# Three blocks per pass, attention of block 1 by DMA transposes, and products of a constant between the H products

## The chip, the cores and the metric

One core of one Trainium2 chip runs the whole program. The metric is the device time of one execution in microseconds (us), as a median of several executions. The engines are TensorE (PE, its weight loads PEld), VectorE (DVE), ScalarE (ACT), GpSimd (POOL) and SyncE (SP), which here only issues DMA transfers.

## The reference

Attention without softmax, RMS norm, and two layers of "mixture" form; everything is float32 in and out.

```python
# q, k, v: 4 batches x 8 heads x 576 positions x 64
kv = einsum('bhsd,bhse->bhde', k, v);  out = einsum('bhsd,bhde->bhse', q, kv)
x = out / sqrt(mean(out*out, -1) + 1e-6) * g_norm       # -> 2304 tokens x 512
h = x @ w_in                                            # 512 x 2048
y = (h * tanh(softplus(h))) @ w_out                     # 2048 x 512
h2 = y @ w2_in                                          # 512 x 1024
z = h2 * softmax(h2);  ln = (z - mean) / sqrt(var + 1e-6) * g_ln
result = ln @ w2_out                                    # 1024 x 512
```

## The kernel before

The 2304 tokens are six blocks of 384. A float32 value is carried as two fp16 parts, high and low, and each product is three fp16 products (high*high, high*low, low*high). A weight matrix arrives in pieces of 512 KB (W1, the first layer's `w_in`, and W2, its `w_out`, 16 pieces each; W3 and W4 for the second layer). Each piece is decoded into its parts by seven steps on three engines: `w_scale` and `w_hi` on ACT, `w_sign` on POOL, `w_low`, `w_put` and `w_lo` on DVE. Five stage buffers hold pieces under way, so a later load on SP waits for the `w_put` of the piece five before it.

PE's work, in order: for each block the attention; "H" products (`h_mm`), 12 matmuls for 128 rows of the hidden layer, 16 such products per block; "Y" products (`y_mm`), also 12 matmuls each; then per tile of 128 tokens a "2" product (`emit_H2`, 24 matmuls of 512 columns) and an "O" product (`emit_O`, the same size), with the layer norm of the tile between them on DVE, ACT and POOL and its result turned by a DMA transpose (`s_T`, tile `lnT`) on the way to O.

Blocks 0 and 1 have their attention in an early form (the functions `e_...`): q is transposed on PE against a unit matrix (`qTp`), multiplied by kv in float32 (`xoT`), mean squares and the norm's factors go through PE as well (`rT`), and the result lands transposed as the two parts `xT` that H reads. Blocks 2 to 5 use the functions `a_...`: q is split on ACT and DVE, turned by a DMA transpose (`qT`), multiplied (`xo`), normed, split, and turned by a second DMA transpose into `xT`. kv itself (`kv_pair`, tile `kvp`) is a sum over positions: 96 partitions of 6 positions, two heads side by side in the 128 columns of the array.

Blocks 0 and 1 first run with the first half of W1 and W2, then with the second half; a partial Y sum is parked by `y_part` on ACT and added later. All other blocks run through whole.

The order on every engine is written by a planner (`Plan.order`). Each task has an engine, a cost in us, the tasks it follows and a lag; PE tasks have due times from a nominal line of H, Y, 2 and O products. The planner takes, per engine, the ready task with the earliest due time, and the instructions stand in the order of the planned times. On the chip each engine then works in that order, whatever the times turn out to be. Before the first H product, gaps in PE's plan of over 1 us get products of zeros (`keep_warm`).

Of the kernel before, what the change touches and what calls it, by code (L numbers as in the profile page):

```python
# [32 lines left out]
class Plan:  # L33
    def __init__(self):
        self.tasks = {}

# [3 lines left out]

    def order(self):
        tasks = self.tasks
        index = {k: n for n, k in enumerate(tasks)}
        followers = {k: [] for k in tasks}
        for k, t in tasks.items():
            for a in t[3]:
                followers[a].append(k)

        seen, topo = set(), []

        def visit(k):
            stack = [(k, iter(tasks[k][3]))]
            seen.add(k)
            while stack:
                at, it = stack[-1]
                for a in it:
                    if a not in seen:
                        seen.add(a)
                        stack.append((a, iter(tasks[a][3])))
                        break  # L60
                else:
                    topo.append(at)
                    stack.pop()

        for k in tasks:
            if k not in seen:
                visit(k)
        due = {}
        for k in reversed(topo):
            d = 1e9 if tasks[k][5] is None else tasks[k][5]  # L70
            for f in followers[k]:
                d = min(d, due[f] - tasks[k][1] - tasks[k][4])
            due[k] = d
        waits = {k: len(t[3]) for k, t in tasks.items()}
# [8 lines left out]
        while True:  # L83
            best = None
            for e, ks in open_.items():
                if ks:
                    at = max(free[e], min(ready[k] for k in ks))
                    if best is None or at < best[0]:
                        best = (at, e)
            if best is None:  # L90
                break
            at, e = best
# [5 lines left out]
            for f in followers[k]:  # L98
                waits[f] -= 1
                ready[f] = max(ready[f], end + tasks[k][4])  # L100
                if not waits[f]:
                    open_[tasks[f][0]].append(f)
        assert len(out) == len(tasks), [k for k in tasks if waits[k] > 0][:20]
# [4 lines left out]
def tile_attn_moe_moe2(  # L108
# [76 lines left out]
    yorder = [(0, 0), (0, 1), (1, 0), (1, 1), (0, 2), (0, 3), (1, 2), (1, 3)]  # L185
    yorder += [(b, g) for b in range(2, NB) for g in range(4)]
# [29 lines left out]
    def load_q(b):  # L216
# [37 lines left out]
    HALF = [slice(0, 64), slice(64, 128)]  # L254

    def kv_full(b, i):

        c = slice(i, i + 1) if b == 0 else slice(0, 4)
        nc.scalar.activation(
            out=kvf[b][HALF[0], c, HALF[0]], in_=kvp_t[b][HALF[0]], func=ACTF.Copy)  # L260
        nc.vector.tensor_copy(out=kvf[b][HALF[1], c, HALF[1]], in_=kvp_t[b][HALF[1]])

    def kv_zero():
        nc.gpsimd.memset(kvr[0], 0.0)

    def kv_hi(b):
        for o in HALF:
            nc.scalar.activation(
                out=kvr[b % 2][o, 0, :, o], in_=kvp_t[b][o], func=ACTF.Copy, scale=32.0)

    def kv_lo(b):
        p = kvp_t[b]
        for o in HALF:
            nc.vector.scalar_tensor_tensor(
                out=kvr[b % 2][o, 1, :, o], in0=p[o], scalar=32.0,
                in1=kvr[b % 2][o, 0, :, o], op0=ALU.mult, op1=ALU.subtract,
# [22 lines left out]
    def e_xo(b, c):  # L299
        qT = eq_t.pop((b, c)).rearrange("p (r t) -> p r t", r=R)  # L300
        p = ex_t[b, c] = psY.tile([128, BLK], FP32, tag=f"y{c % 3}", name="xoT")
        p = p.rearrange("p (r t) -> p r t", r=R)
        for lo, hi, bb in ((0, 128, 0),) if b == 0 else ((0, 64, 0), (64, 128, 1)):
            nc.tensor.matmul(  # L304
                out=p[:, :, lo:hi], lhsT=kvf[bb][:, c], rhs=qT[:, :, lo:hi], start=True, stop=True)
# [6 lines left out]
    def e_ms(b, c):  # L312
        p, tag = (psH, "h") if b == 0 else ((psA, "a"), (psY, "y3"))[c % 2]
        er_t[b, c] = p.tile([128, 512], FP32, tag=tag, name="rT")
# [75 lines left out]
    def a_xo(b, r):  # L390
        qT = qT_t.pop((b, r))
        p = psA.tile([128, H, D], FP32, tag="a", name="xo")
# [157 lines left out]

    def h_mm(b, grp, i, only=None):
        f = (grp * G + i) * 128
        if (b, grp, i) not in h_t:
            h_t[b, grp, i] = psH.tile([128, BLK], FP32, tag="h", name="hp")
# [29 lines left out]
    def y_ends(b, grp):  # L584
        first = grp == 0 or (b < 2 and grp == 2)
        last = grp == 3 or (b < 2 and grp == 1)
# [34 lines left out]
    def y_hi(b, c):  # L621
        if b < 2:
# [5 lines left out]
    def y_lo(b, c):  # L628
        if b < 2:
# [144 lines left out]
    LAND = 1.9  # L774
    load_after = {}

    for n, u in enumerate(PIECES):
        opened = ("open",) if u[0] in "34" else None
        if n < NST:
            before = [("ld", ("1", 0))] if n else [("ld", 0, 3)]  # L780
            before = before[:1] if n >= 0 else [("ldq", 0)]
        else:
            before = [("put", PIECES[n - NST])]
        task(("ld", u), "S", 1.65, w_load, (u,), before + [opened], LAND)
# [23 lines left out]
    KV1 = ("ld", ("1", 3))  # L808
# [7 lines left out]
    for b in range(B):  # L816
        for i in range(4):
            free = []
            if b == 0 and i:
                free = [("ld", 0, i - 1)]  # L820
            if b == 1:
                free = [("ld", 1, i - 1) if i else KV1]
                free += [("kv", 0, i - 2)] if i > 1 else []
            if b == 2:
                free = [("kv", 0, i), ("kv", 1, i + 2) if i < 2 else None]
                free += [("put", ("2", 7))]
            if b == 3:
                free = [("kv", 2, i), ("put", ("2", 15))]
            task(("ld", b, i), "S", 1.8, load_pair, (b, i), free, LAND)

    ring("qhl", 3, ("xo", 1, 3))
    for i in range(4):
        task(("kv", 0, i), "P", 0.9, kv_pair, (0, i),
             [("ld", 0, i)] + ring("a", 1, ("kvf", 0, i)), 0.25)
        task(("kvf", 0, i), "A", 0.3, kv_full, (0, i), [("kv", 0, i), ("zero",)], 0.2)
    for b in range(2):
        task(("ldq", b), "A" if b == 0 else "S", 0.5 if b == 0 else 2.5, load_q, (b,),
             [("qT", 0, c) for c in range(4)] + [KV1] if b else [], 5.0 if b == 0 else LAND)
        if b == 1:
# [246 lines left out]
```

## Time and profile before

| what | us |
|---|---|
| median of 3 runs (640.6 to 642.23) | 641.05 |
| the profiled execution | 646.7 |
| its span, first to last instruction | 644.9 |
| PE busy in the span | 624.8 |

The profiled execution is 1.8 us longer than its span. The page's slices divide the span into 40 stretches of 16.1 us and give the busy share in tenths; the granted clock is 10/10 at 2.4 GHz and 5/10 at 1.2 GHz. A chain of waits follows the last instruction back, at each step to what released it. In a timeline the number in brackets is the idle time of the engine just before the row, and who ended it.

### The profile page before, as it was taken

To read this page: it belongs to the slowest core of one execution; us is meant where nothing else is said; L and a number is where in the kernel's file an instruction comes from. 1 tells how busy PE (TensorE), PEld (TensorE's weight loads), DVE (VectorE), ACT (ScalarE), POOL (GpSimd) and SP (SyncE) were. 2 spreads that over 40 slices of the span, in tenths; PEclk is the share of its full clock that TensorE was granted. 3 is DMA by queue.
4 is the path that set the end of the run, shared out by engine and by line. 5 is a ranking of instruction groups with operands and counts; after the bars stand their busy time and mean duration, and the time that the engine had idled before them with its cause. 6 is when DMAs were issued, how large, how long until landed. Compare 5 with 4: busy or idle time off the path is not lost.

```text
span 644.9 us, 9802 instructions
## 1 busy us (share of the span) xinstructions
PE 624.8 (97%) x4010; PEld 355.0 (55%) x4010; DVE 307.7 (48%) x529; ACT 269.2 (42%) x461; POOL 93.1 (14%) x125
## 2 busy tenths in 40 slices
PE   7899998999999999999999999999999999999995
PEld 5557564666666666666666656665444444444441
DVE  0667887921633144212321239952835555455540
ACT  2568756541523243422332247642523433433340
POOL 1516422100200022001200122500000000000000
PEclk9989798999999999999999999999999999999998
DMA  9985497365340025002200055500342232324322
GB/s 258 270 223 180 134 290 216 80 134 145 66 82 1 1 50 79 4 0 42 41 2 2 17 180 171 188 1 1 66 99 49 66 82 66 83 65 99 77 71 65
DMA packets 92605, 60.41 MB, mean 94 GB/s; under 512 B 65680, under 2 KB 86160, under 8 KB 92560
## 3 DMA queue, kind: packets, MB, share of 16 engines
q1 hardware_dynamic: 91360, 59.00, 36.6%
q10 hardware_dynamic: 1200, 0.79, 0.4%
q8 instruction: 31, 0.51, 0.3%
q14 instruction: 14, 0.11, 0.1%
HBM read 39.33 MB, written 4.72 MB: 68 GB/s over the span
## 4 chain that ended last, share of the span: by engine, by line
PE 89%; DMA 6%; DVE 2%; ACT 2%; issue 1%; POOL 1%; SPq 0%; DVEq 0%; ACTq 0%; POOLq 0%
PE hp L557 27%; PE y L597 26%; PE op L757 15%; PE h L674 14%; DMA st<-in_moe_w_in_dram 2%; PE kvp L246 2%; DMA st<-in_moe_w_out_dram 1%; PE qTp L288 1%; PE xo L398 1%; DMA yT<-in_v_dram 1%; DMA xT<-xhl 1%; PE xoT L304 1%; PE rT L337 1%; DMA lnT<-hl 1%; PE rT L317 1%
## 5 line engine op out<-in xcount | busy, mean ns | idle before, releaser
L597 PE MATMUL y<-g,w 128*128 128x384 f16 x1152 | 204.7, 330 | 2.5 <-ACT yT L610 2.5
L557 PE MATMUL hp<-xT,w 128*128 128x384 f16 x1152 | 201.3, 327 | 3.0 <-ACT w L533 1.9
L597 PEld LDWEIGHTS <-w 128*128 128x128 f16 x1152 | 112.6, 99 | 78.8 <-issue 6.5
L557 PEld LDWEIGHTS <-w 128*128 128x128 f16 x1152 | 111.7, 98 | 78.6 <-ACT w L533 2.2
L567 ACT ACTIVATE m<-hp 128x384 f32<-128x384 f32 x96 | 46.9, 488 | 132.5 <-PE hp L557 131.9
L757 PE MATMUL op<-w,lnT 128*128 128x512 f16 x432 | 97.7, 384 | 4.2 <-DMA lnT<-hl 4.2
L579 DVE SCALAR_TENSOR_TENSOR g<-m,g 128x768 f16<-128x768 f32 x48 | 46.7, 973 | 110.6 <-ACT g L574 110.5
L674 PE MATMUL h<-w,yT 128*128 128x512 f16 x432 | 96.2, 379 | 0.0
L757 PEld LDWEIGHTS <-lnT 128*128 128x128 f16 x432 | 42.6, 99 | 56.5 <-DMA lnT<-hl 4.7
L674 PEld LDWEIGHTS <-yT 128*128 128x128 f16 x432 | 42.3, 98 | 50.4
L510 POOL TENSOR_SCALAR st<-st 128x512 f32<-128x512 f32 x48 | 42.7, 895 | 91.7 <-ACT P L505 71.3
L515 DVE SCALAR_TENSOR_TENSOR st<-st 128x512 int32<-128x512 int32 x48 | 37.1, 787 | 16.8 <-POOL st L510 16.8
L574 ACT ACTIVATE g<-m 128x768 f16<-128x768 f32 x48 | 40.4, 841 | 1.8 <-PE y L597 0.8
L691 ACT ACTIVATE e<-h,nb 128x1024 f32<-128x1024 f32 x18 | 20.1, 1114 | 48.9 <-DVE nb L686 44.4
L505 ACT ACTIVATE P<-st 128x512 f32<-128x512 f32 x48 | 31.9, 673 | 14.2 <-DMA st<-in_moe_w_out_dram 7.8
L522 DVE SCALAR_TENSOR_TENSOR P<-P,st 128x512 int32<-128x512 int32 x48 | 35.6, 759 | 0.2
L418 POOL TENSOR_SCALAR ms<-ms 128x8 f32<-128x8 f32 x12 | 2.6, 216 | 228.2 <-DVE ms L413 228.2
L698 DVE SCALAR_TENSOR_TENSOR z<-h,e 128x1024 f32<-128x1024 f32 x18 | 22.0, 1225 | 21.4 <-ACT e L691 21.4
L724 POOL TENSOR_SCALAR var<-var 128x1 f32<-128x1 f32 x18 | 3.4, 190 | 192.6 <-DVE var L719 192.6
L738 ACT ACTIVATE hl<-z 128x1024 f16<-128x1024 f32 x18 | 19.0, 1056 | 28.9 <-DVE z L733 28.9
L705 ACT ACTIVATE e<-z,nmz 128x1024 f32<-128x1024 f32 x18 | 20.7, 1147 | 23.7 <-DVE nmz L701 23.7
L742 DVE TENSOR_TENSOR hl<-z,hl 128x1024 f16<-128x1024 f32 x18 | 22.0, 1224 | 15.7 <-ACT hl L738 15.7
(96 smaller groups left out, 421.6 us busy)
## 6 DMA issues: line engine op xcount, KB each, us to landing
st<-in_moe_w_in_dram SPq DMA_DIRECT2D x24, 512.0 KB, 6.7
st<-in_moe_w_out_dram SPq DMA_DIRECT2D x24, 512.0 KB, 4.3
yT<-in_k_dram SPq DMA_DIRECT2D x16, 288.0 KB, 7.9
yT<-in_v_dram SPq DMA_DIRECT2D x16, 288.0 KB, 8.1
out_dram<-osb SPq DMA_DIRECT2D x18, 256.0 KB, 2.0
qraw<-in_q_dram SPq DMA_DIRECT2D x3, 768.0 KB, 6.3
qraw<-in_q_dram SPq DMA_DIRECT2D x4, 384.0 KB, 8.6
qraw<-in_q_dram ACTq DMA_DIRECT2D x1, 768.0 KB, 6.9
```

The lines of the kernel that those rows point to most:

```text
L505: nc.scalar.activation(out=P, in_=v[:, :, 1], func=ACTF.Copy, scale=2.0 ** -111)
L510: nc.gpsimd.tensor_scalar(out=v[:, :, 1], in0=v[:, :, 1], scalar1=0.0, scalar2=1.0, op0=ALU.mult, op1=ALU.mult)
L515: nc.vector.scalar_tensor_tensor(out=v[:, :, 0], in0=v[:, :, 0], scalar=29, in1=v[:, :, 1], op0=ALU.logical_shift_right, op1=ALU.bitwise_or)
L522: nc.vector.scalar_tensor_tensor(out=P.bitcast(I32), in0=P.bitcast(I32), scalar=3, in1=v[:, :, 0], op0=ALU.logical_shift_left, op1=ALU.bit ...
L557: nc.tensor.matmul(out=h_t[b, grp, i], lhsT=w1[:, c, wa, f:f + 128], rhs=xT_t[b][:, C * xa + c], start=(c == 0 and m == 0), stop=(c == C - ...
L567: nc.scalar.activation(out=m_t[b, grp, i // 2][:, i % 2], in_=h_t.pop((b, grp, i)), func=ACTF.Mish, scale=2.0 ** -16)
L574: nc.scalar.activation(out=g_t[b, grp][:, 0, 2 * i:2 * i + 2], in_=m_t[b, grp, i], func=ACTF.Copy, scale=64.0)
L579: nc.vector.scalar_tensor_tensor(out=g_t[b, grp][:, 1, j], in0=m_t.pop((b, grp, i)), scalar=64.0, in1=g_t[b, grp][:, 0, j], op0=ALU.mult, ...
L597: nc.tensor.matmul(out=y_t[cc][:, 0:BLK], lhsT=w2[:, grp * G + ii, wa, cc * 128:(cc + 1) * 128], rhs=g_t[b, grp][:, ga, ii], start=(first ...
L674: nc.tensor.matmul(out=hp[:, half], lhsT=y[:, c, ya, tok], rhs=w3[:, c, wa, half * 512:(half + 1) * 512], start=(m == 0), stop=(m == 3 * C ...
L698: nc.vector.scalar_tensor_tensor(out=z, in0=T[t, "hp"], scalar=2.0 ** -14, in1=T[t, "e"], op0=ALU.mult, op1=ALU.mult, accum_out=sz)
L757: nc.tensor.matmul(out=op, lhsT=lnT[:, K2 * la + kk], rhs=w4[:, kk, wa], start=(m == 0), stop=(m == 3 * K2 - 1),)
```

## The change

Block 1's attention takes the form `a_...`; only block 0 keeps the early form. k and v are laid on 128 partitions of 9 positions, one head of a pair on partitions 0 to 63 and the other on 64 to 127 (`load_pair`, `kv_pair`). Three blocks instead of two (`NI = 3`) run through the first half of the weights before the second half, and Y follows H's order of blocks. The first loads on SP stand in a fixed line, q of block 0 first. The planner runs twice, the second time with the first plan's times as due times. `keep_warm` multiplies the unit matrix, 256 columns at a time, and now also fills planned gaps of over 0.5 us after the first H product, up to a planned time of 150, in the bank of the next H product.

```diff
+    NI = 3
...
-    units = [(0, 0), (0, 1), (1, 0), (1, 1), (0, 2), (1, 2), (0, 3), (1, 3)]
-    units += [(b, g) for b in range(2, NB) for g in range(4)]
...
-    line = ["H", "H", "H", "Y", "H", "Y", "Y"]
+    units = [(b, 2 * half + g) for half in range(2) for b in range(NI) for g in range(2)]
+    units += [(b, g) for b in range(NI, NB) for g in range(4)]
+    line = ["H", "H", "H"]
     while line.count("H") < NU:
-        line += ["H", "Y"]
-    hs, ys = iter(units), iter(yorder)
+        line += ["Y", "H"]
+    hs, ys = iter(units), iter(units)
...
-        t = yT[(0 if b == 1 else 2) + i].rearrange("p c a t -> p (c a t)").bitcast(FP32)[0:KP]
-        raw[b, i] = t.rearrange("p (a h r d) -> p a h r d", a=2, h=2, r=KR)
+        t = yT[RAW[b][i]].rearrange("p c a t -> p (c a t)").bitcast(FP32)
+        raw[b, i] = t[:, 0:2 * KR * D].rearrange("p (a r d) -> p a r d", a=2, r=KR)
...
-                in_=src[b, 2 * i:2 * i + 2].rearrange("h (p r) d -> p h r d", r=KR),
+                in_=src[b, 2 * i:2 * i + 2].rearrange("h (p r) d -> (h p) r d", r=KR),
...
-            (nc.scalar if b == 0 else nc.sync).dma_start(
+            nc.sync.dma_start(
...
-                    lhsT=t[:, 0, h, r],
-                    rhs=t[:, 1, h, r],
+                    lhsT=t[HALF[h], 0, r],
+                    rhs=t[HALF[h], 1, r],
...
-        p = psA.tile([128, H, D], FP32, tag="a", name="xo")
+        p, tag = (psY, f"y{r}") if b == 1 else (psA, "a")
+        p = p.tile([128, H, D], FP32, tag=tag, name="xo")
...
         if r == 0:
-            xT_t[b] = xt_p.tile([128, 2 * C, BLK], FP16, tag="xT", name="xT")
+            if b == 2:
+                xT_t[b] = yT[NB - 1].rearrange("p c a t -> p (c a) t")
+            else:
+                xT_t[b] = xt_p.tile([128, 2 * C, BLK], FP16, tag="xT", name="xT")
...
-    LAND = 1.9
+    LAND, PAIR, QLD, PIECE = 2.0, 2.15, 3.0, 1.6
...
-    for b in range(2):
-        task(("ldq", b), "A" if b == 0 else "S", 0.5 if b == 0 else 2.5, load_q, (b,),
...
+    tiles = [(b, r) for b in range(1, NB) for r in range(R)]
+    for b in range(1, NB):
...
-    zeros = kvr[1].rearrange("p a c d -> p (a c d)")
-
-    def keep_warm(n):
+    any_ = ident.bitcast(FP16)
+
+    def keep_warm(n, p):
         for _ in range(n):
             nc.tensor.matmul(
-                out=warm, lhsT=zeros[:, 0:128], rhs=zeros[:, 0:512], start=True, stop=True)
+                out=p[:, 0:256], lhsT=any_[:, 0:128], rhs=any_[:, 0:256], start=True, stop=True)
+
+
+    w, kv = (lambda f: ("ld", ("1", f))), (lambda b, i: ("ld", b, i))
+    plan.line([
+        ("ldq", 0), kv(0, 0), kv(0, 1), w(0), kv(0, 2), kv(0, 3), w(1), w(2), w(3),
+        ("ldq", 1), kv(1, 0), kv(1, 1), w(4), kv(1, 2), w(5), kv(1, 3), w(6), w(7),
+    ])
...
+    for at_time, key in plan.order():
+        if plan.tasks[key][5] is not None:
+            plan.tasks[key][5] = at_time
     order = plan.order()
...
-            if not heated and at_time - free > 1.0:
-                keep_warm(int((at_time - free - 0.4) / 0.25))
+            gap = at_time - free
+            if not heated and gap > 1.0:
+                keep_warm(int((gap - 0.4) / 0.12), warm)
+            elif heated and gap > 0.5 and at_time < 150:
+                keep_warm(int((gap - 0.2) / 0.12), h_open(h_line[0]))
```

The planner writes new orders for every engine. The end of ACT's program before, from the layer norm of the second last tile on (`hl` is a tile's normed result, `osb` the copy of a finished O product):

```order
375 L765 ACTIVATE osb<-op 128x512
376 L738 ACTIVATE hl<-z 128x1024
377 L691 ACTIVATE e,S__5660<-h_5589,nb 128x1024
378 L705 ACTIVATE e,sq<-z,nmz 128x1024
379 L765 ACTIVATE osb<-op 128x512
380 L738 ACTIVATE hl<-z 128x1024
381 L691 ACTIVATE e,S__5745<-h_5674,nb 128x1024
382 L705 ACTIVATE e,sq<-z,nmz 128x1024
383 L765 ACTIVATE osb<-op 128x512
384 L738 ACTIVATE hl<-z 128x1024
385 L765 ACTIVATE osb<-op 128x512 x2
```

and now:

```order
367 L726 ACTIVATE hl<-z 128x1024
368 L679 ACTIVATE e,S__5738<-h_5660,nb 128x1024
369 L693 ACTIVATE e,sq<-z,nmz 128x1024
370 L753 ACTIVATE osb<-op 128x512
371 L726 ACTIVATE hl<-z 128x1024
372 L679 ACTIVATE e,S__5823<-h_5745,nb 128x1024
373 L753 ACTIVATE osb<-op 128x512
374 L693 ACTIVATE e,sq<-z,nmz 128x1024
375 L726 ACTIVATE hl<-z 128x1024
376 L753 ACTIVATE osb<-op 128x512 x6
```

Behind the last tile's normed result stood two copies of O products, now six; on PE the last "2" product is followed by three O products before and by seven now, since the 2 products have moved ahead among the last Y products.

SP's program from its start before (`yT_104` to `yT_107` receive k and v of block 0, `st` weight pieces, `yT_102` the first pair of the next batch):

```order
1 L209 DMA yT_104<-in_k_dram 96x2x384
2 L209 DMA yT_104<-in_v_dram 96x2x384
3 L209 DMA yT_105<-in_k_dram 96x2x384
4 L209 DMA yT_105<-in_v_dram 96x2x384
5 L209 DMA yT_106<-in_k_dram 96x2x384
6 L209 DMA yT_106<-in_v_dram 96x2x384
7 L209 DMA yT_107<-in_k_dram 96x2x384
8 L209 DMA yT_107<-in_v_dram 96x2x384
9 L460 DMA st<-in_moe_w_in_dram 128x4x256 x4
10 L209 DMA yT_102<-in_k_dram 96x2x384
```

and now, from the seventh piece of W1 on (`qT` and `xT` are the two transposes of a tile of block 1):

```order
23 L441 DMA st<-in_moe_w_in_dram 128x4x256
24 L363 DMA_TRANSPOSE qT<-qhl 128x8x128
25 L441 DMA st<-in_moe_w_in_dram 128x4x256
26 L363 DMA_TRANSPOSE qT<-qhl 128x8x128 x2
27 L449 DMA st<-in_moe_w_out_dram 128x1024 x2
28 L209 DMA qraw<-in_q_dram 128x8x192
29 L449 DMA st<-in_moe_w_out_dram 128x1024 x2
30 L427 DMA_TRANSPOSE xT<-xhl 128x8x128
31 L449 DMA st<-in_moe_w_out_dram 128x1024 x2
32 L427 DMA_TRANSPOSE xT<-xhl 128x8x128
33 L363 DMA_TRANSPOSE qT<-qhl 128x8x128
34 L449 DMA st<-in_moe_w_out_dram 128x1024
```

Twelve transposes for blocks 1 and 2 now stand among the weight loads of the first two layers; before, the first transpose on SP stood behind the last of these loads.

PE's program where the products of the constant stand for the first time behind an H product (line 999, three of them, between two rows of block 0's norm factors):

```order
77 L314 MATMUL rT<-ident,rho 64x128 x6
78 L999 LDWEIGHTS ident
79 L999 MATMUL hp<-ident 128x256
80 L999 LDWEIGHTS ident
81 L999 MATMUL hp<-ident 128x256
82 L999 LDWEIGHTS ident
83 L999 MATMUL hp<-ident 128x256
84 L314 MATMUL rT<-ident,rho 64x128 x6
85 L545 LDWEIGHTS w_68
```

The same pairs stand 25 times at the program's start, 20 times ahead of the eighth H product, 29 times ahead of the first Y product, 11 times behind it, and 9 times ahead of block 1's first Y product. On PE's line to the first Y product block 1's `qTp`, `xoT` and `rT` matmuls are gone, and three `xo` of 24 matmuls stand there.

## Rows read from the trace of the kernel before

**Rows 1.** The page, parts 1 and 2: engines' busy time; 40 slices in tenths.

```profile
PE 624.8 (97%) x4010; PEld 355.0 (55%) x4010; DVE 307.7 (48%) x529; ACT 269.2 (42%) x461; POOL 93.1 (14%) x125
PE   7899998999999999999999999999999999999995
PEclk9989798999999999999999999999999999999998
```

**Rows 2.** The chain of waits at its end: start, us, what.

```profile
614.60 5.18 PE h L674 x24
619.78 10.23 PE op L757 x48
630.01 4.29 DMA lnT<-hl
634.35 7.00 PE op L757 x24
```

**Rows 3.** The chain of waits, first 120 us.

```profile
9.08 4.62 PE qTp L288 x48
15.90 0.77 PE rT L317 x6
18.27 0.75 PE xoT L304 x2
19.03 0.80 PE rT L337 x12
20.59 0.85 PE kvp L246 x24
66.91 3.95 PE y L597 x12
114.36 1.95 PE y L597 x12
```

**Rows 4.** Timeline of PE, single rows; from the span's start.

```profile
1.44 3.17 PE L1027 MATMUL idle<-kvr 128*128 128x512 f16 x7 [1.44 <-DVE ones L1040]
65.37 1.55 PE L337 MATMUL rT<-ident,rho 128*64 128x128 f32 x12 [0.93 <-POOL rho L329]
108.66 3.76 PE L597 MATMUL y<-g,w 128*128 128x384 f16 x12 [2.52 <-ACT yT L610]
242.44 0.83 PE L398 MATMUL xo<-kvr,qT 128*128 128x128 f16 x12
249.05 0.87 PE L398 MATMUL xo<-kvr,qT 128*64 128x128 f16 x24
```

**Rows 5.** Stretches: busy us of each engine, granted clock, DMA share, GB/s.

```profile
0.00:40.00 40.00, 32.49 (x340) 22.05 (x342) 15.07 (x35) 16.23 (x33) 11.37 (x17) 0.96 1.04 265
40.00:60.00 20.00, 20.00 (x185) 13.84 (x183) 15.26 (x26) 16.18 (x33) 8.61 (x9) 1.00 0.60 196
64.30:71.00 6.70, 5.77 (x28) 3.11 (x27) 5.13 (x8) 4.69 (x9) 4.03 (x5) 0.50 0.24 81
108.70:112.00 3.30, 3.30 (x11) 1.57 (x11) 3.30 (x6) 3.30 (x8) 0.57 (x1) 0.50 0.50 179
634.40:637.70 3.30, 3.30 (x8) 1.13 (x9) 0.00 (x0) 0.00 (x0) 0.00 (x0) 0.50 0.00 0
```

**Rows 6.** Decoding's last step for W2, and ACT before it.

```profile
L540 DVE TENSOR_TENSOR w<-P,w x2: 684/684/685, 58.4 to 62.8; 128x512 f16<-128x512 f32 x2
35.74 0.49 ACT L296 ACTIVATE qT<-qTp 128x384 f32<-128x384 f32 x1 [2.21 <-PE qTp L288]
```

**Rows 7.** Transposes of block results: issue, and landing over all twelve.

```profile
248.83 1.23 SPq L446 DMA_TRANSPOSE xT<-xhl  x1
DMA to landing us min/median/max: 3.0/3.1/5.0
```

**Rows 8.** Weight pieces of W1: landing; q of block 0 on the page.

```profile
DMA to landing us min/median/max: 3.7/7.1/12.6
qraw<-in_q_dram ACTq DMA_DIRECT2D x1, 768.0 KB, 6.9
```

More of the change, by code (lines that the diff above doesn't have):

```diff
@@ L39, in add, with line @@
         self.tasks[key] = [engine, cost, fn, [a for a in after if a is not None], lag, due]
+    def line(self, keys):
+        for a, b in zip(keys, keys[1:]):
+            self.behind.setdefault(b, []).append(a)
     def order(self):
@@ L43, in order @@
         index = {k: n for n, k in enumerate(tasks)}
+        edges = {k: [(a, tasks[a][4]) for a in t[3]] + [(a, 0.0) for a in self.behind.get(k, ())]
+                 for k, t in tasks.items()}
         followers = {k: [] for k in tasks}
[L45 to L67, printed above, removed]
+        for k, es in edges.items():
+            for a, lag in es:
+                followers[a].append((k, lag))
+        waits = {k: len(es) for k, es in edges.items()}
+        topo = [k for k in tasks if not waits[k]]
+        for k in topo:
+            for f, _ in followers[k]:
+                waits[f] -= 1
+                if not waits[f]:
+                    topo.append(f)
+        assert len(topo) == len(tasks), [k for k in tasks if waits[k] > 0][:20]
         due = {}
         for k in reversed(topo):
[L70 to L74, printed above, removed]
+            due[k] = 1e9 if tasks[k][5] is None else tasks[k][5]
+            for f, lag in followers[k]:
+                due[k] = min(due[k], due[f] - tasks[k][1] - lag)
+        waits = {k: len(es) for k, es in edges.items()}
         ready = {k: 0.0 for k in tasks}
@@ L299, in e_xo @@
     def e_xo(b, c):
-        qT = eq_t.pop((b, c)).rearrange("p (r t) -> p r t", r=R)
+        qT = eq_t.pop((b, c))
         p = ex_t[b, c] = psY.tile([128, BLK], FP32, tag=f"y{c % 3}", name="xoT")
[L302 to L305, printed above, removed]
+        nc.tensor.matmul(out=p, lhsT=kvf[0][:, c], rhs=qT, start=True, stop=True)
     def e_sq(b, c):
@@ L584, in y_ends @@
     def y_ends(b, grp):
-        first = grp == 0 or (b < 2 and grp == 2)
-        last = grp == 3 or (b < 2 and grp == 1)
+        first = grp == 0 or (b < NI and grp == 2)
+        last = grp == 3 or (b < NI and grp == 1)
         return first, last
@@ L881, in tile_attn_moe_moe2 @@
-    kv_after = {2: [("kvz",)], 3: [("xo", 2, r) for r in range(R)]}
-    order_a = [2] + [(2, r) for r in range(R)] + [3] + [u for u in tiles if u[0] > 2]
+    task(("ldq", 0), "S", QLD, load_q, (0,), (), LAND)
+    for c in range(4):
+        u = (0, c)
+        bank = f"y{c % 3}"
+        task(("qT", *u), "P", 0.95, e_qT, u,
+             [("ldq", 0), ("ident",)] + ring(bank, 1, ("qc", *u)), 0.25)
+        task(("qc", *u), "A", 0.49, e_qc, u, [("qT", *u)] + (
+            ring("qT", 3, ("xo", *u)) if c < 3 else ring("xhl", 2, ("xo", *u))))
@@ L890, in tile_attn_moe_moe2 @@
+    for b in range(B):
+        every = [("kvf", 0, i) for i in range(4)] + [("zero",)] if b == 0 else [
+            ("kv", b, i) for i in range(4)]
+        if b:
+            plan.tasks["kv", b, 0][3] += bank_a[b]
+        if b > 1:
+            every += [("xo", b - 1, r) for r in range(R)]
+        task(("kvh", b), "A", 0.75, kv_hi, (b,), every)
         task(("kvl", b), "V", 0.8, kv_lo, (b,), [("kvh", b)])
@@ L904, in tile_attn_moe_moe2 @@
         task(("xlo", *u), "V", 0.7, a_xlo, u, [("xhi", *u)])
-        gone = [("H", b - 2, 3, i) for i in range(G)]
+        gone = [("kv", 0, 3)] if b == 2 else [
+            ("H", {3: 0, 4: 1, 5: 3}[b], 3, i) for i in range(G)] if b > 2 else []
         task(("xT", *u), "S", 1.3, a_xT, u,
@@ L923, in tile_attn_moe_moe2 @@
             else:
-                x = [("xlo", b, c) for c in range(C)] if b < 2 else [
+                x = [("xlo", b, c) for c in range(C)] if b == 0 else [
                     ("xT", b, r) for r in range(R)]
@@ L953, in tile_attn_moe_moe2 @@
                 for c in range(C) if turn else (j,):
-                    bank += last_of.get(c, [rings[f"y{c}"][-1]])
+                    bank += last_of.get(c, rings.get(f"y{c}", [])[-1:])
             task(("Y", b, grp, j), "P", 12 * MM, y_mm,
@@ L975, in tile_attn_moe_moe2 @@
                 else:
[L976 removed]
+                    raws = [("kv", 3, i) for i in range(4)] if b < 5 else [("H", 2, 3, i) for i in range(G)]
                     task(("yhi", b, c), "A", 0.49, y_hi, (b, c), end + raws)
```

167 lines of the change are left out of this document (63 added, 104 removed).

## The prediction

> **What bounds the kernel now.** I read the page first: PE is busy for 624.8 of 644.9 us, and its row of slices dips only in the first, around the third and fifth, the seventh, and the last; the granted clock dips beside it [rows 1]. So the kernel is PE's work plus what PE waits or runs slowly at both ends of the program. Then the chain of waits at the end, then its first 120 us, then PE's timeline and the stretches by clock.
>
> At the end the last "2" product (5.18 us) is followed by two O products, then PE waits for the last tile's transposed norm, and the last O product takes 7.00 us [rows 2], because it begins at half the clock [rows 5].
>
> At the start PE works through block 0's attention, then H products of the first weights mixed with block 1's attention. The last piece of that is an `rT` that waits on POOL, and right behind it the first Y product begins at 66.91 us [rows 3, 4]. It takes 3.95 us against 1.95 for twelve such matmuls later on [rows 3]: the stretch 64.3 to 71.0 runs at 0.50, 1.2 GHz, after PE had stood idle between its `rT` rows [rows 4, 5]. At 108.66 PE had waited 2.52 us for ACT's copy of the partial sum, and twelve matmuls take 3.76 us at 0.50 [rows 4, 5]. From 112 us to 630 us I see no loss that matters. The DMA engines are full for the first 40 us, 265 GB/s at a share of 1.04, and no longer after [rows 5].
>
> **The change, part by part,** against the profiled execution: 646.7 us, 1.8 us over its span of 644.9.
>
> *The tail.* Seven O products follow the last "2" product instead of three. The last tile's norm and transpose took from 619.78 to 634.30 (10.23 + 4.29) [rows 2]; six O products now lie beside it, 6 x 5.18 = 31.1 us. The wait of 634.35 - 630.01 = 4.3 us goes, and with it the slow clock, 7.00 - 5.18 = 1.8 us. What follows the last matmul stays. **Gain 6.1 us.** Nothing else is late then: each of these O products needs only a tile finished earlier.
>
> *The way to the first Y product.* PE's order now gives a lower end, if it never waits. 25 constants of 256 columns; seven of 512 took 3.17 us from 1.44 on [rows 4], so 25 x 0.227 = 5.7, to 7.1 us. (q lands by then: it took 6.9 us while it shared the engines with k and v [rows 8]; now it goes first.) Then up to the first H matmul: q's transposes 4.62; four `xoT` x 0.75 = 3.0; three rounds of mean squares x 0.77 = 2.3; two of factors x 0.80 = 1.6 [rows 3]; and four `kvp`.
>
> For `kvp` no row shows the new form. Before, 24 records took 0.85 us [rows 3], 35.4 ns each; now there are 36 (9 x 2 x 2). At the same 35.4 ns that is 1.28 us. The low end is the old 0.85, if a record of 64 rows takes less than one of 96. The high end is two heads that don't overlap: `xoT` in full width takes 0.75 us for two records of 384 columns [rows 3], 0.98 ns a column, so 36 x 64 x 0.98 = 2.26 us. I take 1.28: the heads still write two different halves of the columns, as in that row.
>
> The Trainium skill, "TensorEngine Tiling (Array Packing)", section Restrictions and Gotchas, says that different row tiles cannot access one PSUM bank at the same time. The two heads of the new `kvp` are two row tiles of one bank, so by that rule they would take turns, near the 2.26 us; no row here shows two row tiles, and the sum goes by 1.28.
>
> So four `kvp` are 5.1 us, and the first H matmul stands at 7.1 + 16.6 = 23.7. From there to the first Y product: eight H products x 1.95 = 15.6 [rows 3], four `kvp` 5.1, what is left of block 0's norm 0.77 + 2 x 0.80 = 2.4, three `xo` of 24 matmuls. Such a one begins at 249.05 and the next row at 249.85 by its pitch of 0.81 us, 0.87 with its modelled end [rows 4]: 2.5. And 3 + 20 + 29 = 52 constants: 5.18 us for 24 of 512 columns [rows 2] is 0.108 for 256 columns, 5.6 us. Together 31.2: **the first Y at 54.9 us at the earliest.**
>
> The upper end is the first piece of W2. In SP's order the bytes up to it are q of two blocks 1.57 MB, k and v of two batches 4.72, nine pieces 4.72, three transposes 0.79: 11.8 MB, at 265 GB/s 44.5 us. Before, 11.0 MB stood there, 41.6 us, and the piece was decoded at 58.4 + 0.7 = 59.1 [rows 6], 17.5 us later. The same 17.5 us would make it 62.0. Part of that lag goes: ACT then stood in its queue behind copies that waited on PE's transposes of q for block 1 (2.21 us at one of them) [rows 6], and those are gone. In place of them ACT, DVE and POOL get block 1's tiles: from an `xo` to its transpose 248.83 - 242.44 = 6.4 us, and 3.0 to 5.0 to land [rows 4, 7]. With DVE busy 15.26 of 20 us there [rows 5] I take the middle, **58.0: a gain of 8.9 us**, between 4.9 and 12.0.
>
> *The clock at the first Y.* With 29 constants right ahead PE does not stand idle, so 3.95 - 1.95 = **2.0 us gained**; nothing if the wait outlasts them.
>
> *What PE gets after the first Y.* 20 more constants, 2.2 us lost unless they lie in a wait. Block 1's `xT` is covered: behind its last `xo` stand two H, three Y, 60 constants and an `xo`, 3.9 + 5.9 + 6.5 + 0.7 = 17 us, against 6.4 + 5.0. Block 2's is just covered: behind its last `xo` three Y, nine constants and two Y, 5 x 1.95 + 1.0 + 0.7 = 11.4 us, against 9.4 to 11.4. With queues I take 1.0 us. **Loss 3.2 us**, up to 6.
>
> *The wait at 106 to 112.* It was ACT's copy of block 0's partial sum, late among the decoding of the second half. With three blocks in the first half that half is due later by eight H and eight Y products, 16 x 1.95 = 31 us, and the copy's place in PE's order has nine constants in it, already counted. **Gain** 2.52 + 3.76 - 1.95 = **4.3 us.**
>
> *`kvp` of the later batches*: eight, on PE's full line, 8 x 0.43 = **3.4 us lost**, between 0 and 11.3.
>
> k and v with longer runs, the second plan, and the loads in line have their effect in the first Y's time; I cost them at nothing more, since 265 GB/s is what the mixture gave before.
>
> Sum: 6.1 + 8.9 + 2.0 - 3.2 + 4.3 - 3.4 = 14.7 us. The profiled execution would be 632.0. It lies 5.65 us over the median of the runs, 641.05; taking that off gives **626.4 us**.
>
> **Rivals.**
>
> *The weights come no sooner.* The first Y stays at 66.9, with DVE and ACT decoding as late as before. For it: W1's pieces land no earlier, byte for byte. Against: block 1's detour over PE, on which they waited, is gone. 626.4 + 8.9 = 635.3.
>
> *The heads of `kvp` take turns.* 2.26 us each: 8 x 0.98 = 7.8 more on the line; at the start 7.8 more on PE, of which some 4 show. 638.2. For it: no row shows two row tiles. Against it: the overlap of column halves in the old row. This is what the Trainium skill's rule above would give.
>
> *Transposes behind loads: slower.* SP works in order, and twelve transposes now stand among loads; those of W1's pieces took up to 12.6 us to land, against 3.1 for a transpose in an empty queue [rows 7, 8]. Each of blocks 1 and 2 has two in series, `qT` and `xT`. At 12.6 each is 9.5 us late: block 1 loses 19 - 5.6 of cover = 13.4, block 2 some 9.5 as its `qT` can go ahead: 22.9, 649 us. It decides from a landing of about 9 us on. Against it: after 40 us the engines have room, 196 GB/s [rows 5], and most of the twelve are issued there. The Trainium skill, "DMA: Bandwidth & Descriptors", section Queues, rings and completion order, has each engine consume descriptors in ring order; by that rule the first three, among full queues, would be late.
>
> *The constants only cost.* Where PE arrives late its data is there, and 72 x 0.108 = 7.8 us are pure work; 5.6 of them are in my earliest 54.9 already, so at the most 4 us more: 630.4.
>
> **How the numbers follow.** The forecast gets 0.62, late weights 0.15, `kvp` in turns 0.12, late transposes 0.07, constants 0.04. The forecast's own range is 619 to 632 (first Y at its ends, `kvp` at 0.85 or 1.28). With late weights and most of `kvp` in turns it is 618 to 637. A measurement tells about 0.3%, 1.9 us, from no change. Faster: 0.62 + 0.15 + 0.04 and 0.09 of `kvp`, 0.90; same 0.03, the rest of `kvp`; slower 0.07, the transposes.
>
> **What would show it.** In the changed profile: no idle PE before the last O product, at full clock; the first Y near 58 us at 1.95 us; `kvp` at 1.28 us for 36 records; idle PE at most 1 us ahead of block 2's first H; no half clock between 40 and 630 us. It is wrong if a `kvp` takes 2 us, if transposes land in 9 us or more, or if the first Y stands behind 62.

## The result and the profile after

The changed kernel takes 633.02 us (median of four runs, 632.43 to 633.46); the kernel before, beside it, 641.64 (640.6 to 644.08). The ratio is 0.986 with a 95% interval of 0.983 to 0.989. The forecast was 626.4, in a range of 618 to 637: the direction is right, the gain is 8.6 us and not 14.7. The profiled execution of the changed kernel took 633.35 us (span 631.6), against 632.0 worked out for it.

The page after, to be read against [rows 1]:

```profile
PE 618.8 (98%) x4221; PEld 355.4 (56%) x4221; DVE 309.9 (49%) x534; ACT 269.7 (43%) x459; POOL 99.4 (16%) x126
PE   8999988999999999999999999999999999999997
PEclk9999999999999999999999999999999999999999
```

The row of the clock has no dip left. PE has more matmuls (211 more) and less busy time, since no stretch behind its first constants runs at half the clock. The end of the chain of waits answers to [rows 2]:

```profile
585.91 5.18 PE h L662 x24
591.09 36.27 PE op L745 x168
```

Seven O products in one piece: the wait of 4.29 us and the slow one of 7.00 us are gone. PE's timeline at the start answers to [rows 3, 4]; in brackets is the idle time ahead of the row and what ended it:

```profile
1.34 4.38 PE L999 MATMUL idle<-ident 128*128 128x256 f16 x25 [1.34 <-POOL ident L1012]
6.75 2.34 PE L269 MATMUL qTp<-ident,qraw 128*64 128x128 f32 x36 [1.02 <-DMA qraw<-in_q_dram]
27.10 1.26 PE L233 MATMUL kvp<-yT 64*64 64x64 f32 x36
28.30 3.59 PE L545 MATMUL hp<-xT,w 128*128 128x384 f16 x21
...
51.01 3.33 PE L999 MATMUL hp<-ident 128*128 128x256 f16 x29
54.17 0.49 PE L585 MATMUL y<-g,w 128*128 128x384 f16 x2
55.40 1.80 PE L585 MATMUL y<-g,w 128*128 128x384 f16 x10 [0.73 <-DVE w L521]
57.03 1.36 PE L999 MATMUL hp<-ident 128*128 128x256 f16 x11
58.23 0.49 PE L585 MATMUL y<-g,w 128*128 128x384 f16 x2
58.87 1.80 PE L585 MATMUL y<-g,w 128*128 128x384 f16 x10
...
61.17 2.35 PE L585 MATMUL y<-g,w 128*128 128x384 f16 x12
63.58 7.97 PE L545 MATMUL hp<-xT,w 128*128 128x384 f16 x48
...
84.72 0.83 PE L376 MATMUL xo<-kvr,qT 128*128 128x128 f16 x12 [0.79 <-DVE xf L403]
91.23 1.15 PE L999 MATMUL hp<-ident 128*128 128x256 f16 x9
94.00 4.06 PE L585 MATMUL y<-g,w 128*128 128x384 f16 x24 [1.62 <-ACT yT L598]
99.86 11.86 PE L545 MATMUL hp<-yT,w 128*128 128x384 f16 x72 [1.80 <-DMA yT<-xhl]
```

A `kvp` of 36 records ends 1.20 us after its start (27.10 to 28.30). The first Y begins at 54.17, against 66.91, at full clock; with the wait of 0.73 us inside it, its twelve matmuls end at 57.03. Three waits of 4.2 us together stand behind it, the last for block 2's transposed input (`yT<-xhl` here is that input in a borrowed tile), and nothing after 100 us.

### The profile page after: what moved, and what is told of

Same layout as the page of the kernel before. It is cut to its first block, busy times and chain, and to the rows that moved or that the text cites. A ratio compares the mean times of both kernels' runs of the same rounds, so it can differ in the third digit from the quotient of the medians.

```text
span 631.6 us, 10239 instructions
## 1 busy us (share of the span) xinstructions
PE 618.8 (98%) x4221; PEld 355.4 (56%) x4221; DVE 309.9 (49%) x534; ACT 269.7 (43%) x459; POOL 99.4 (16%) x126
## 4 chain that ended last, share of the span: by engine, by line
PE 86%; DMA 5%; DVE 3%; POOL 2%; ACT 2%; issue 1%; SPq 0%; POOLq 0%; DVEq 0%; ACTq 0%
PE y L585 27%; PE hp L545 26%; PE op L745 15%; PE h L662 15%; DMA qraw<-in_q_dram 3%; PE kvp L233 3%; POOL rho L398 1%; PE xo L376 1%; DVE P L503 1%; DMA yT<-xhl 1%; DMA st<-in_moe_w_in_dram 1%; POOL st L491 1%; DVE st L496 1%; PE qTp L269 0%; ACT P L486 0%
## 5 line engine op out<-in xcount | busy, mean ns | idle before, releaser
L585 PE MATMUL y<-g,w 128*128 128x384 f16 x1152 | 200.6, 326 | 2.6 <-ACT yT L598 1.6
L545 PE MATMUL hp<-xT,w 128*128 128x384 f16 x960 | 165.1, 326 | 0.1
L745 PE MATMUL op<-w,lnT 128*128 128x512 f16 x432 | 95.2, 379 | 0.0
L491 POOL TENSOR_SCALAR st<-st 128x512 f32<-128x512 f32 x48 | 45.3, 950 | 97.8 <-ACT P L486 95.6
L396 POOL TENSOR_SCALAR ms<-ms 128x8 f32<-128x8 f32 x15 | 6.3, 421 | 220.9 <-DVE ms L391 220.4
L496 DVE SCALAR_TENSOR_TENSOR st<-st 128x512 int32<-128x512 int32 x48 | 35.8, 760 | 10.3 <-POOL st L491 10.2
L545 PE MATMUL hp<-yT,w 128*128 128x384 f16 x192 | 33.0, 326 | 1.8 <-DMA yT<-xhl 1.8
L673 DVE TENSOR_REDUCE mx<-h 128x1 f32<-128x1024 f32 x18 | 22.0, 1223 | 20.6 <-PE h L662 20.6
L686 DVE SCALAR_TENSOR_TENSOR z<-h,e 128x1024 f32<-128x1024 f32 x18 | 22.0, 1224 | 17.5 <-ACT e L679 17.5
```

Of the source, the lines that this page charges most:

```text
L491: nc.gpsimd.tensor_scalar(out=v[:, :, 1], in0=v[:, :, 1], scalar1=0.0, scalar2=1.0, op0=ALU.mult, op1=ALU.mult)
L496: nc.vector.scalar_tensor_tensor(out=v[:, :, 0], in0=v[:, :, 0], scalar=29, in1=v[:, :, 1], op0=ALU.logical_shift_right, op1=ALU.bitwise_or)
L545: nc.tensor.matmul(out=h_t[b, grp, i], lhsT=w1[:, c, wa, f:f + 128], rhs=xT_t[b][:, C * xa + c], start=(c == 0 and m == 0), stop=(c == C - ...
L585: nc.tensor.matmul(out=y_t[cc][:, 0:BLK], lhsT=w2[:, grp * G + ii, wa, cc * 128:(cc + 1) * 128], rhs=g_t[b, grp][:, ga, ii], start=(first ...
L673: nc.vector.reduce_max(out=mx, in_=T[t, "hp"], axis=AX.X)
L745: nc.tensor.matmul(out=op, lhsT=lnT[:, K2 * la + kk], rhs=w4[:, kk, wa], start=(m == 0), stop=(m == 3 * K2 - 1),)
```

## The experiments

Each kernel is timed beside the kernel before. The changed kernel hardly varies, so its variants are set against its own median, 633.0. It was timed on two of the four occasions on which runs were made; on the other two the comparison rests on that steadiness, while the kernel before had medians from 641.55 to 643.7.

**1. How steady is the kernel before?** First unchanged, with a new profile:

> The kernel before, unchanged, with a new profile; its profiled execution so far took 646.7 us against a median near 641. Theory 1 (some of the losses in that profile are not in a usual execution): the new profiled execution lies near 641, and a wait or a half-clock stretch that the first profile shows (first Y at 66.91 taking 3.95 us, twelve matmuls at 108.66 taking 3.76 us after 2.52 us idle, the last O after 4.29 us idle) is shorter by some 5 us together. Theory 2 (a profiled execution is simply longer by about 5 us): the new one lies near 646 with the same stretches. Rival to both: near 641 with all these stretches as before, and the 5 us elsewhere (the loads at the start, or matmuls that are all a little slower).

It took 643.48 us (12 runs, 641.24 to 646.58). Over the 61 runs of it made in this study the median is 643.1, from 640.2 to 647.6. This profiled execution took 643.74; the first had taken 646.7. Its PE timeline where the first had the idle 2.52 us of [rows 4]:

```profile
107.46 2.11 PE L597 MATMUL y<-g,w 128*128 128x384 f16 x12 [0.95 <-ACT yT L610]
109.40 2.11 PE L557 MATMUL hp<-xT,w 128*128 128x384 f16 x12
67.17 4.02 PE L597 MATMUL y<-g,w 128*128 128x384 f16 x12
```

The wait is 0.95 us instead of 2.52, and the twelve matmuls behind it take 1.94 (107.46 to 109.40) instead of 3.6 (108.66 to 112.25). The spans differ by 3.0 us, and that place accounts for it. The first Y (last row) and the tail are as they were. So theory 1 holds in part: one place gives 3.0 us, not 5, and the execution lies at 643.74, not near 641. The 4.3 us that I counted for the wait at 106 to 112 is worth about 1 us in this execution. For 57 of these runs the granted clock is listed: the 12 with 0.992 or more all took under 642.2 us, the 14 at 645.0 or above all had 0.987 or less. The reverse doesn't hold (0.987 stands beside 641.4 as well), so the clock goes with the spread and doesn't explain every run.

The changed kernel, again unchanged:

> The changed kernel, unchanged, beside as many runs of the kernel before on the same chip, where that took 641.2 to 646.6, median 643.7. Theory 1 (the kernel before varies from run to run at waits that are long enough in some runs to bring the slow clock, and the changed one has none of these left): 632 to 634, median 633.0, a spread under 2 us, ratio 0.983, so 10.7 us of gain. Rival (this chip is slower than the one of the first runs for either kernel): 635.0 to 635.5, ratio 0.986 as before.

632.93 us (632.14 to 633.45), beside 641.55 (640.36 to 646.29) on that occasion: 0.985, 0.982 to 0.988. The changed kernel varies by 1.3 us and the kernel before by 7, and the time is the one that theory 1 gave; its ratio of 0.983 did not come, because the kernel before was at 641.55 again. Against the median of all its runs, 643.1, the gain is 10.2 us.

**2. The tail, one part alone.** In the kernel before:

```diff
-        pe += [("O", t - 3), ("2", t)] if t < NT2 - 1 else [("2", t)]
-    pe += [("O", t) for t in range(NT2 - 4, NT2)]
+        pe += [("O", t - 8), ("2", t)] if t > 7 else [("2", t)]
+    pe += [("O", t) for t in range(NT2 - 8, NT2)]
```

> The kernel before with one part of the change: seven O products behind the last 2 product instead of three (O placed five steps later in the nominal line), nothing else moved. By the sum of the prediction the wait of 4.3 us and 1.8 us of slow clock go: 6.1 us less, about 635. Rival 1, the tail's loss is smaller in a usual execution: 3 us or less, 638 or more. Rival 2, the last tile's norm is late again because more O evictions stand in ACT's queue ahead of it: no gain, 641.

636.11 us (634.27 to 640.9), ratio 0.9895 (0.9855 to 0.9935) to the 643.7 beside it: 6.8 us less, within 4.2 to 9.3. And the old tail in the changed kernel:

```diff
+    plan.line([("O", NT2 - 4), ("2", NT2 - 1)])
```

> The changed kernel with the old tail: the last 2 product is put behind the fourth last O product, so that three O products follow it. By the sum 4.3 us of wait and 1.8 us of half clock ahead of and in the last O product come back: 633.0 + 6.1 = 639. Rival, the clock does not fall there any more: 633.0 + 4.3 = 637.3. If the tail was not worth anything in a usual execution: 633.

639.01 us (637.81 to 639.23), 6.1 more than 632.93. Its chain of waits ends as [rows 2] do:

```profile
610.80 10.23 PE op L745 x48
621.03 4.27 DMA lnT<-hl
625.34 7.05 PE op L745 x24
```

The term of 6.1 us is right from both sides.

**3. The constants.** Those behind the first H product left out:

```diff
-            elif heated and gap > 0.5 and at_time < 150:
-                keep_warm(int((gap - 0.2) / 0.12), h_open(h_line[0]))
```

> The changed kernel without the 72 products of a constant behind the first H product (the 25 ahead of the attention stay). Theory of the prediction: most of them lie in waits, so PE stands idle in their place; the first Y comes at 54 to 55 us as before, but after an idle stretch of some 5 us it and its neighbours run at 0.50, which costs about 2 us at each place where that happens: 633 to 637. Rival 1, they only cost: 72 x 0.108 = 7.8 us less, down to 625. Rival 2, they neither cost nor give: 633 within 1 us, with the clock full all the same.

633.07 us (631.92 to 633.6): no difference, rival 2, but not with the full clock that I had put beside it. The timeline:

```profile
52.89 0.50 PE L585 MATMUL y<-g,w 128*128 128x384 f16 x2 [2.69 <-ACT w L514]
55.27 5.26 PE L585 MATMUL y<-g,w 128*128 128x384 f16 x22 [1.88 <-DVE w L521]
60.37 0.83 PE L376 MATMUL xo<-kvr,qT 128*128 128x128 f16 x12
...
63.71 7.97 PE L545 MATMUL hp<-xT,w 128*128 128x384 f16 x48 [0.30 <-DMA xT<-xhl]
```

PE stands idle where the constants were, and 22 matmuls of Y take 5.1 us (55.27 to 60.37), 1.5 more than 22 at the full clock's 0.1625 us each. Yet the first H of block 1 begins at 63.71, against 63.58, because it waits for its transposed input. The constants buy clock in a stretch whose end is set elsewhere.

**4. The layout of k and v.** In the changed kernel, all batches as before (`wide(b)` says which batches take the new layout, here none):

```diff
+    def wide(b):
+        return not (True)
...
-        raw[b, i] = t[:, 0:2 * KR * D].rearrange("p (a r d) -> p a r d", a=2, r=KR)
+        if wide(b):
+            raw[b, i] = t[:, 0:2 * KR * D].rearrange("p (a r d) -> p a r d", a=2, r=KR)
+        else:
+            raw[b, i] = t[0:KP].rearrange("p (a h r d) -> p a h r d", a=2, h=2, r=K6)
...
-                in_=src[b, 2 * i:2 * i + 2].rearrange("h (p r) d -> (h p) r d", r=KR),
+                in_=pair.rearrange("h (p r) d -> (h p) r d", r=KR) if wide(b)
+                else pair.rearrange("h (p r) d -> p h r d", r=K6),
...
-                    lhsT=t[HALF[h], 0, r],
+                    lhsT=t[HALF[h], 0, r] if wide(b) else t[:, 0, h, r],
```

> The changed kernel with k and v of all batches on 96 partitions as before (6 positions to a partition, 24 records to a kvp), all else in the same order. A kvp falls from 1.20 to 0.85 us: 8 x 0.35 = 2.8 us less on PE's full line; the eight at the start lie ahead of the wait for weights. Theory 1: the k and v transfers with shorter runs take longer (landing 7.9 and 8.1 us before against 4.6 and 5.0), so the weight pieces behind them come about 3 to 4 us later and the first Y with them: 633.0 - 2.8 + 3.5 = 633.7. Rival 1, the layout makes no difference to the weights: 630.2. Rival 2, nothing of kvp shows because waits take it up: 633 or more, with the first Y where it is.

635.85 us (634.44 to 638.83), 2.9 more although the eight later `kvp` are shorter: theory 1 in kind, but with 5.7 us lost at the start and not 3.5. What DMA moved in the first 36 us, in 40 slices, the kernel before, this one, and the changed kernel:

```profile
GB/s 0 10 181 335 329 327 293 291 273 273 266 266 275 261 273 328 332 338 358 332 350 348 266 256 183 174 173 189 208 262 254 285 312 324 339 250 232 217 292 227
GB/s 0 0 73 257 300 312 190 327 297 289 263 265 320 268 270 280 285 273 286 310 348 348 338 199 198 185 163 178 233 219 235 288 271 259 254 263 228 221 243 251
GB/s 0 0 95 269 260 289 219 323 407 392 383 412 407 410 390 389 353 350 347 296 194 213 201 208 286 369 345 332 370 389 373 387 361 367 312 323 172 48 24 119
```

Where k and v load first, in the slices from 7 to 14 us, the old layout moves 261 to 320 GB/s in either kernel, the new one 383 to 412. The profile of the old layout has waits of 0.3 to 0.8 us between 7 and 19 us, and then half the clock:

```profile
20.00:40.00 20.00, 19.34 (x128) 0.55 1.11 234
62.33 0.49 PE L596 MATMUL y<-g,w 128*128 128x384 f16 x2
63.55 1.80 PE L596 MATMUL y<-g,w 128*128 128x384 f16 x10 [0.73 <-DVE w L532]
47.23 1.00 SPq L460 DMA_DIRECT2D st<-in_moe_w_out_dram  x2
DMA to landing us min/median/max: 4.2/4.2/4.2
```

The first Y comes 8.2 us later, with the same 0.73 us of wait for a weight inside it. That weight's piece, the first of W2, is issued at 47.23 and lands at 51.4, 8.1 us later than in the changed kernel (43.3), and its last step of decoding begins 11 us after the landing in both. Ahead of its load on SP stand block 1's three transposes of q, and the last of them is off SP only at 47.1, against 38.1. So the load is held up in SP's program; that the slow PE holds up the transposes is the likely reading, which no run isolates. (This profile is of the longest of its runs, at a mean clock of 0.983; in the shorter ones the clock is 0.993 to 0.997, so the slow stretch is likely shorter there, and the 8 us are not those of a median run.)

Then the new layout for batches 0 and 1 alone, in the changed kernel (all else of the edit as above):

```diff
+    def wide(b):
+        return not (b > 1)
```

> The changed kernel with the 128-partition layout for batches 0 and 1 alone, whose loads stand ahead of the first weights, and the old 96 partitions for batches 2 and 3. Theory: eight later kvp at 0.85 in place of 1.20 us on a line that never waits, 2.8 us less: 630.2, below both kernels. Rival: their slower loads delay weights or transposes between 60 and 110 us, and the waits at 94 and 100 us grow by as much: 632 to 634.

629.73 us (629.02 to 629.95), ratio 0.980 (0.977 to 0.983): 3.2 less than the changed kernel, 2.8 expected, and the shortest time of all. A later `kvp` here and in the changed kernel:

```profile
198.60 0.92 PE L244 MATMUL kvp<-yT 96*64 96x64 f32 x24
199.40 1.26 PE L233 MATMUL kvp<-yT 64*64 64x64 f32 x36
```

The layout alone in the kernel before:

```diff
-    KP = 96
-    KR = S // KP
+    KR = 2 * S // 128
...
-                    lhsT=t[:, 0, h, r],
+                    lhsT=t[64 * h:64 * h + 64, 0, r],
```

> The kernel before with one part of the change: k and v of all batches on 128 partitions of 9 positions, nothing else moved. Price: 8 later kvp x 0.35 = 2.8 us on PE's full line. Theory 1 (undoing the layout in the changed kernel cost 2.9 us in all, 2.9 + 2.8 = 5.7 us of it at the start, so it gains that here too): 641.6 - 5.7 + 2.8 = 638.7, with the wait of 2.9 us for v and the slower clock between 20 and 40 us gone. Rival (the start of the kernel before is held by block 1's early attention and the weights behind it, and the first Y stays near 67): 641.6 + 2.8 = 644.4.

644.42 us (642.5 to 646.34), ratio 1.0024 (1.000 to 1.0047). Early DMA is as fast as in the changed kernel (up to 410 GB/s), and still the first Y stands where it stood:

```profile
64.80 1.28 PE L336 MATMUL rT<-ident,rho 128*64 128x128 f32 x12 [0.98 <-POOL rho L328]
67.81 2.47 PE L596 MATMUL y<-g,w 128*128 128x384 f16 x12
```

The rival holds: W2's first piece lands at 41.3, against 44.7, and its last step of decoding still begins at 59.7, against 58.4. Even so PE comes to the first Y only at 67.81, from block 1's early attention with its waits for POOL: the weight isn't what it waits for. With the mixed layout and the long tail in the kernel before (the nominal line of experiment 2, and):

```diff
+    def wide(b):
+        return b < 2
```

> The kernel before with the two parts that have shown a gain, and no other: seven O products in the tail, and the 128-partition layout for batches 0 and 1 alone. Theory 1 (these two are the whole gain): 641.6 - 6.5 - 5.7 = 629.4, as fast as the changed kernel with the mixed layout (629.7). Rival (the first Y does not move, see the run on the layout alone): 641.6 - 6.5 = 635.1. Between them, about 632, if the layout gains half: the rest then belongs to block 1's new attention form and the order of the loads.

636.92 us (635.2 to 638.05), ratio 0.9903 (0.9865 to 0.9941), no better than the tail alone (636.11, 0.9895). Theory 1 falls: in this kernel faster loads are worth nothing clear of noise without the new start.

**5. The other parts of the start, undone.** Two blocks through the first half:

```diff
-    NI = 3
+    NI = 2
```

> The changed kernel with two blocks instead of three through the first half of the weights (NI = 2), the planner doing the rest. The second half of W1 and W2 is due 16 x 1.95 = 31 us earlier. Theory: the waits around 106 to 112 us of the kernel before come back, 2.5 to 4.3 us or more, partly filled with constants: 636 to 641. Rival: the waits are in the copies and not in the number of blocks, so 632 to 634. What speaks for less than both: block 2's transposed input is then needed later, and the 1.8 us wait for it at 100 us goes: 631.

632.51 us (632.13 to 632.89): three blocks are worth nothing. PE's longest waits of this kernel behind its start; for ACT's copy it is 0.8 us, at 98.63, and not 2.5:

```profile
PE hp L545 <- DVE w L523: 1.5, 1, 1.5
PE hp L545 <- DMA xT<-xhl: 1.4, 1, 1.4
PE y L585 <- ACT yT L598: 0.8, 1, 0.8
```

The planner run once:

```diff
-    for at_time, key in plan.order():
-        if plan.tasks[key][5] is not None:
-            plan.tasks[key][5] = at_time
```

> The changed kernel with the planner run once (the first plan's times are not used as due times); PE's order up to some 150 us and around the changes of half is another, the tail and the first loads are the same. Theory: the waits between 46 and 100 us stand elsewhere but are set by the same decoding of weights: 632 to 635. Rival: the second plan is what made the start tight, 636 or more.

637.62 us (636.62 to 638.03), 4.7 more: the rival holds. Block 2's first H now waits 4.45 us, and 48 matmuls behind it take 9.3 instead of 7.8:

```profile
98.45 9.42 PE L545 MATMUL hp<-yT,w 128*128 128x384 f16 x48 [4.45 <-DMA yT<-xhl]
107.71 2.11 PE L585 MATMUL y<-g,w 128*128 128x384 f16 x12
```

That is 4.45 + 1.46 against 1.80 us, 4.1 of the 4.7. And the fixed line of first loads left out:

```diff
-    plan.line([
-        ("ldq", 0), kv(0, 0), kv(0, 1), w(0), kv(0, 2), kv(0, 3), w(1), w(2), w(3),
-        ("ldq", 1), kv(1, 0), kv(1, 1), w(4), kv(1, 2), w(5), kv(1, 3), w(6), w(7),
-    ])
```

> The changed kernel without the fixed line of first loads: all of batch 0's k and v stand before the first weights, batch 1's and the last two before the fourth to eighth weight piece; q of block 0 is still first. Theory (the decoding of the weights on DVE and ACT ends last before the first Y, and it follows the landing of the pieces): later pieces by three pairs, 1.8 MB at 265 GB/s = 6.7 us at most, about half of it seen: 635 to 638. Rival (decoding is held by what stands ahead of it in the queues of DVE and ACT, not by the landing): 633 within 1 us.

635.04 us (634.03 to 635.63), 2.1 more: the lower end of the theory. There PE took other work first (the first Y at 67.34), so the landing of the weights and the order that the planner made of it aren't told apart.

## Why the prediction was right in direction and 6.6 us too low

Against the profiled execution the sum was nearly right: 14.7 us forecast, 646.7 - 633.35 = 13.35 measured. Part of that is luck: the gain at the first Y came out 2.9 us larger and the loss behind it 3.2 us larger. Step by step:

- *The tail*, 6.1: 6.8 and 6.1 in the two experiments. Right.
- *The first Y*, 8.9: too small. Its twelve matmuls end at 57.03; without their 1.95 us it counts as 55.1, which is 11.8 us gained. What it waits for is the last step of decoding of W2's first piece. The load of that piece before, with the time to its landing, then what stands on SP from 28 us now, the same load, its landing, and the decoding ([rows 6] had 58.4):

```profile
34.98 0.35 SPq L468 DMA_DIRECT2D st<-in_moe_w_out_dram  x1
DMA to landing us min/median/max: 9.7/9.7/9.7
28.11 4.27 SPq L363 DMA_TRANSPOSE qT<-qhl  x1
32.48 0.53 SPq L441 DMA_DIRECT2D st<-in_moe_w_in_dram  x1
33.19 4.91 SPq L363 DMA_TRANSPOSE qT<-qhl  x2
38.19 1.00 SPq L449 DMA_DIRECT2D st<-in_moe_w_out_dram  x2
DMA to landing us min/median/max: 5.1/5.1/5.1
L521 DVE TENSOR_TENSOR w<-P,w x24: 669/678/1155, 54.2 to 391.2; 128x512 f16<-128x512 f32 x24
```

  The piece landed at 44.7 before and at 43.3 now; the prediction's count of bytes gave 41.6 and 44.5. From landing to decoded it took 14.4 us before and 11.6 now, where the prediction had 17.5 before, and 13.5 now by its choice of 58.0. So of the 3.1 us between 58.0 and the decoded piece at 54.9, 1.9 are this lag, which was counted from a landing worked out and not read, and 1.2 are the landing. That the landing came so near is luck. The step "265 GB/s is what the mixture gave before" failed, since loads ran at up to 410; and the load stood behind three transposes, at which SP spent most of 28.11 to 38.1 while DMA fell to 24 GB/s, which the count left out. With the old layout in the same order the piece landed at 51.4.
- *The clock at the first Y*, 2.0: the full clock is there, and without the constants 22 matmuls lose 1.5 us of it again. But the total doesn't change without them, since block 1's first H then waits for its transposed input: as a gain in time the term isn't shown.
- *After the first Y*, -3.2: too small a loss. 20 constants take 2.2, and the waits 0.79 + 1.62 + 1.80 = 4.2 us, where I had given 1.0: -6.4. The tiles of blocks 1 and 2 pass POOL, DVE and ACT beside the weights' decoding, and the chain of waits goes there between 47 and 100 us; some of its pieces:

```profile
47.40 1.65 POOL rho L398
89.53 1.98 POOL rho L398
94.11 5.62 DMA yT<-xhl
```

- *The wait at 106 to 112*, 4.3: there in the first profile, about 1 us in the second. The reason given, that three blocks make the second half due later, fell: with two blocks 0.8 us of it come back, and with three blocks PE waits 1.62 us for such a copy at 94.00.
- *`kvp`*, -3.4: -2.8 by the rows (8 x 0.35), 3.2 by the clock of the runs. The heads don't take turns: 36 records in 1.20 us are 33.3 ns each, against 35.4 for the old ones [rows 3], where turns would have given 2.26 us. In the trace's single records from 27.1 us on, the matmuls of the two heads start 7 ns apart, and the next pair 58 ns after them. The Trainium skill, "TensorEngine Tiling (Array Packing)", section Restrictions and Gotchas, says that different row tiles cannot access one bank at the same time; here two row tiles did overlap, with their results on partitions 0 to 63 and 64 to 127 of one bank, and the measurement decides.

These terms make 6.1 + 11.8 + 2.0 - 6.4 + 4.3 - 2.8 = 15.0. Of the 1.65 us by which that is too much, 0.7 is the end behind the last matmul (644.9 - 641.35 = 3.55 us before, 631.6 - 627.36 = 4.24 after), against "What follows the last matmul stays". Most of the other 1 us stands in the rows of the result: 0.3 us between 58.23 and 58.87, where two matmuls take 0.33, and 0.5 between 61.17 and 63.58, where twelve take 1.95.

The step that failed is the last: "It lies 5.65 us over the median of the runs, 641.05; taking that off". This treats the excess as the same in both kernels. It belongs to the kernel before: its profiled execution was one of its long ones, with a stretch in it that the change removes (3.0 us of it shown in experiment 1). The changed kernel's profiled executions, 633.35 and 633.03, lie 0.3 and 0.1 over their medians. So the same microseconds were counted twice, once as a gain and once taken off. 5.3 us of the miss are this, and 1.35 the sum. Not all of the 5.65 was such an excess: the profiled execution lies 3.6 us over the median of the 61 runs, and the other 2.1 are a median of three runs that was low.

The rivals: the first Y did come sooner; the heads of `kvp` overlap; "the constants only cost" is out, since without them the time is the same. Transposes behind loads did not decide: the twelve of `xT` landed in 3.0 to 5.6 us and the fifteen of `qT` in 3.0 to 8.8 (the next row), under the 9 us from which that rival counted. The 8.8 is the one of 28.11, and 4.27 of it are SP's time at its issue, where most take 1.2. Nearest to that rival is block 2's last input, which landed 5.62 us after its issue while PE waited 1.80 for it.

```profile
DMA to landing us min/median/max: 3.0/3.2/8.8
```

What no rival had is the reverse, weight loads that stand behind the transposes.

Where the gain is: of 10.2 us between the medians of all runs, 6 to 7 are the tail, and about 3 are paid for `kvp`; the start gives the rest, 6 to 7. Its parts don't add. Undone one at a time in the changed kernel, the layout costs 2.9 + 2.8 = 5.7, the second plan 4.7, the line of loads 2.1, three blocks and the constants nothing; the layout alone in the kernel before gains less than its price. The new attention form of block 1 alone was not tried, nor were the transposes moved behind more of the weight loads, so their shares stay open.

## What to carry to other kernels

Before a sum against one profiled execution is turned into a median, profile the kernel twice: where the profiled execution lies above the median, the excess is likely in the stretches that vary, and a change that removes these must not have it taken off again. A constant that keeps the clock up is worth its place only where the stretch behind it ends the chain. Use a layout that loads faster where loads are waited for, and the one that computes faster where they aren't: mixing the two beat both kernels. Read a landing from the trace where it stands there, rather than counting bytes, and look for what a load stands behind in its engine's program.

## What was not expected of the hardware

Loading k and v as 128 partitions of one run of 2304 bytes moved 383 to 412 GB/s, as 96 partitions of two runs of 1536 bytes 261 to 320, with the same bytes; which of the two, partitions or length of run, makes the difference wasn't told apart. Two row tiles of 64 rows, with their results on different partitions of one bank, overlapped at 33.3 ns a record. An idle 0.95 us, or 1.99 in the run with the long tail, left the next twelve matmuls at full clock (1.94 us); after 2.52 us they took 3.6. The kernel before, which has such a place, took 640.2 to 647.6 us in 61 runs; how much of that this place makes, beyond the 3.0 us between two of them, the runs don't tell. It isn't all of it: with the layout alone in the kernel before, the longest of its twelve runs, 646.34 us, has only 0.18 us of idle there, and its runs still spread over 3.8 us.
